# Attention, a mixture of experts and a dense layer: all engines in source order from the experts on, second-layer splits over 21 units, y's low parts on VectorE

## The chip, the cores and the metric

The kernel runs on one core of a Trainium2 chip. The metric is the device time of one execution in microseconds, the median of several runs. A core has five engines with instruction queues of their own, each of which runs its instructions in the order in which the compiled program lists them: TensorE (PE, matmuls; its weight loads are listed as PEld), VectorE (DVE), ScalarE (ACT), GpSimd (POOL) and SyncE (SP, which issues most DMAs). They wait for each other by semaphores.

## The reference

Three layers follow each other on 2 x 768 tokens of 512 numbers, all in fp32.

```python
scores_l_m = np.where(mask_l, scale * q @ k.T, -1e9)        # a window of 16 tokens
scores_s = scale * q @ k_sum.T + np.log(block)              # 24 block maxima of k
a = softmax(concatenate([scores_l_m, scores_s]))
x = a @ concatenate([v, v_sum])                             # (1536, 512)

expert_idx = np.argmax(xn @ en.T / tau, axis=1)             # 8 experts
for e in range(E):
    h = np.maximum(x[mask] @ w1[e], 0.0)                    # 512 -> 1024
    out[mask] = gate_w[mask, None] * (h @ w2[e])            # 1024 -> 512

h = np.maximum(x @ w_in, 0.0)                               # 512 -> 2048
return h * h @ w_out                                        # 2048 -> 512
```

## The kernel before

An fp32 operand of a matmul is split into a high part (rounded to fp32r) and a low part (the rest); three products of parts make up one product (`SPLIT`, `SPLIT2`). A split is always a cast on ACT and a subtraction on DVE or POOL, which needs the cast.

The kernel has three stretches. Up to about 90 us it computes the attention, whose output x is kept in `x_hl` and stored to the DRAM tile `xall`. Then come the experts. For each batch the expert that most tokens chose is applied to all tokens of the batch, 384 tokens (a group) at a time; that is `expert_units(b, gi)`. Tokens of other experts are gathered in blocks of 128: the first block is `first_block`, inside the stream; further ones would run in a loop at the end. At last comes layer two (`layer_units`), with 4 groups.

**Units.** Experts and layer two are cut into units: unit f of a group computes the first product for 128 hidden numbers (`h` or `z`, 12 matmuls), its activation (`hh` for the experts, `r` and `sq` for layer two), and the second product (`ya`, 12 matmuls, or `oa`, 9 or 12), which accumulates over f. `push(unit)` issues a unit's first half and then the second half of the unit before. So there are 16 units for each batch's experts and 64 for layer two. Counted through, units 0 to 15 belong to batch 0, 16 to 31 to batch 1, and layer two starts at 32.

**Beside the units** run generators, of which `tick()` lets each of four queues do one step, twice per unit: `route` (which expert each token takes), `plan` (the blocks), `first_block` (which calls `extra`: one-hot tiles `pt` and the sums `pi`, the gather of the rows `xe`, a transpose to `xet`, then eight steps f with `st_x`, `phe`, `he`, `ye` and `pye`) and `finish(gi)`. The last adds the block's outputs to a group's expert outputs by four matmul pairs `pd`, and makes y, layer two's input, from the sums: add on DVE (line 874), cast on ACT (875), low part on POOL (876). The banks of `pd` come from the pool `psm`, which has two.

**Layer two's weights** are 32 halves (`wm`, n = 0 to 31, two to a hidden slice). They lie in DRAM as 64-bit floats and are loaded as `sm`; DVE decodes them in three steps (lines 896, 900, 903) into `d`, and a split follows (927 on ACT, 928 on DVE). The odd halves from 9 on are decoded early and put back to DRAM (`put_by`, tile `wd`), to be loaded again as `dl` when they are split. Loads `st`, `st_x` and `sm` share the four slots of the pool `stg`.

**The order.** Two regions follow each other, attention, and the rest. In both `manual_schedule` is given PE alone: PE runs in the order of the source, and a scheduler orders the other engines by priority; `high_priority` lifts activations. `split(ns)` and `put_by(ns)` are called between units: half 0 before unit 16, halves 1 to 7 in units 16 to 22, two each in units 26 to 33 (8 to 23), and two each in units 39 to 42 (24 to 31).

Of the kernel before, what the change touches and what calls it, by code (L numbers as in the profile page):

```python
# [22 lines left out]
P = 128  # L23
# [4 lines left out]
E = 8  # L28
# [53 lines left out]
def program(ctx, tc, a):  # L82
# [411 lines left out]
    def plan():  # L494
# [15 lines left out]
        for e in range(E):  # L510
            v.tensor_tensor(
                out=st[:, e + 1 : e + 2], in0=st[:, e : e + 1], in1=nb[:, e : e + 1], op=ALU.add
            )
        cb = xt.tile([P, 24, E], F32, tag="xt", name="cb")
# [15 lines left out]
            out=rk, in0=pr, in1=st[:, :E].unsqueeze(1).to_broadcast([P, n, E]), op=ALU.add  # L530
# [3 lines left out]
        v.tensor_scalar(out=posx, in0=posx, scalar1=-1.0, scalar2=None, op0=ALU.add)  # L534
        gf = gate.rearrange("p b j -> p (b j)")
# [104 lines left out]
    region.enter_context(tc.manual_schedule(engines={ET.PE}))  # L640
# [98 lines left out]
    def extra(i, ei, pos, new, res):  # L739
# [32 lines left out]
        v.tensor_scalar(out=xe, in0=xe, scalar1=ge[:, 2:3], scalar2=None, op0=ALU.mult)  # L772
        yield 6
# [59 lines left out]
    def first_block():  # L833
# [8 lines left out]
        s.copy(ye[:, 0], pye)  # L842
        v.tensor_tensor(out=ye[:, 1], in0=pye, in1=ye[:, 0].bitcast(F32), op=ALU.subtract)
# [4 lines left out]
    def finish(gi):  # L848
# [17 lines left out]
        for m in range(NC_):  # L866
# [9 lines left out]
            g.tensor_tensor(  # L876
# [8 lines left out]

    def decoded(n):

        f, o = divmod(n, 2)
        st = stg.tile([P, DM, 2], U32, tag="stg", name=f"sm{n}")
        nc.sync.dma_start(  # L890
            st.rearrange("p n w -> p (n w)"),
            a["wm"][f].bitcast(U32)[:, o * 2 * DM : (o + 1) * 2 * DM],
        )
# [14 lines left out]
    def put_by(ns):  # L908
        for n in ns:
            words[n] = dram.tile([P, DM], U32, name=f"wd{n}")  # L910
            g.dma_start(words[n], decoded(n))

    def split(ns):

        for n in ns:
# [3 lines left out]
            if n in words:  # L919
                d = dp.tile([P, DM], U32, tag="dl", name=f"dl{n}")  # L920
                nc.sync.dma_start(d, words[n])
            else:
                d = decoded(n)
            df = d.bitcast(F32)
# [7 lines left out]
    weights(0, range(4, NF1))  # L932
# [9 lines left out]

    by = list(range(9, 2 * NF2, 2))

    def put_next():
        if by:
            put_by([by.pop(0)])

    for n, unit in enumerate(expert_units(0, 0)):
        push(unit)  # L950
        if n >= 3:
            put_next()
    while not planned:
        tick()
    X2.close()
    w1p = pool("w1p", 8, side="right")
    weights(1, range(4))
    for n, unit in enumerate(expert_units(0, 1)):
        push(unit)
        put_next()  # L960
        if 2 <= n < 6:
            weights(1, [n + 2])
    slots = [w2p] * 8 + [w1p] * 8 + [w0] * 8
    split([0])
    u1 = [expert_units(1, gi) for gi in range(2)]
    for n, unit in enumerate(u1[0] + u1[1]):
        push(unit)
        if n < 7:
            split([n + 1])
        elif n >= 10:  # L970
            split([2 * n - 12, 2 * n - 11])


    def layer_units(gi):
        st = {}

        def first(f):
# [58 lines left out]
    for n, unit in enumerate(units[:7]):  # L1036
        push(unit)
        if n < 2:
            split([2 * n + 20, 2 * n + 21])
    while queues["rows"] or queues["ends"]:  # L1040
        tick()
    Y2.close()
    w3p = pool("w3p", 8)
    for n, unit in enumerate(units[7:]):
        if n + 12 < NF2:
            split([2 * n + 24, 2 * n + 25])
        push(unit)
# [5 lines left out]
    with tc.For_i(1, n, 1) as i:  # L1053
# [7 lines left out]
        s.copy(yr, pye)  # L1061
# [90 lines left out]
```

## Time and profile before

| | |
|---|---|
| median of 3 runs | 531.59 us (530.61 to 531.60) |
| the profiled execution, its own time | 534.48 us |
| its span, first to last instruction | 532.5 us |
| mean granted clock of TensorE | 0.988 |
| PE busy | 504.7 us (95%) |
| DVE busy | 280.9 us (53%) |
| ACT busy | 196.8 us (37%) |
| POOL busy | 72.6 us (14%) |

The profile comes from one execution and gives times from the first instruction on. A timeline lists start and duration of instructions, like ones merged ("x12"); in brackets stands the idle time before them and what ended it. Instructions of one engine overlap a little in the records, so that from one start to the next is often less than the duration. A wait is put down to what came last. The granted clock is the share of TensorE's full speed that was granted.

### The profile page before, as it was taken

The numbers are of one execution on the slowest core, as the hardware profiler recorded it, in microseconds if no ns is written. First come the engines' busy times: TensorE is split into PE (matmuls) and PEld (weight loads), VectorE is DVE, ScalarE is ACT, GpSimd is POOL, SyncE is SP. The second block draws the span as 40 slices with busy tenths as digits, with TensorE's granted clock in tenths as the row PEclk, the third lists the DMA queues.
The fourth block names the chain that finished last, engine by engine and source line by source line (L and its number), as shares of the span: only waits on it lengthen the run. The fifth ranks groups of instructions, "written<-read, shape, count | busy, mean of one in ns | idle before, by whom it ended". The sixth has DMA issues, their size and how long they took to land.

```text
span 532.5 us, 9937 instructions
## 1 busy us (share of the span) xinstructions
PE 504.7 (95%) x3921; PEld 458.5 (86%) x3922; DVE 280.9 (53%) x761; ACT 196.8 (37%) x454; POOL 72.6 (14%) x77
## 2 busy tenths in 40 slices
PE   6988988999997999999999999999999999999994
PEld 3777777999996988999989999999999999999993
DVE  2875879866866769599825423222232222322221
ACT  4576678314232432344636322222222222222221
POOL 1345234010012230213202000000000000000000
PEclk9898999999998999999999999999999999999999
DMA  8945647744798657254100001000010000100001
GB/s 252 266 131 173 218 158 243 248 168 160 214 340 281 200 203 237 66 178 136 42 1 20 2 0 60 0 1 0 1 59 1 1 0 2 60 1 0 1 0 65
DMA packets 18033, 55.80 MB, mean 105 GB/s; under 512 B 2151, under 2 KB 3571, under 8 KB 17982
## 3 DMA queue, kind: packets, MB, share of 16 engines
q1 hardware_dynamic: 16942, 51.71, 30.4%
q0 software_dynamic: 1040, 3.41, 1.6%
q8 instruction: 33, 0.54, 0.4%
q14 instruction: 18, 0.15, 0.1%
HBM read 45.66 MB, written 9.44 MB: 103 GB/s over the span
## 4 chain that ended last, share of the span: by engine, by line
PE 73%; DVE 10%; DMA 8%; ACT 4%; issue 2%; POOL 1%; SPq 1%; ACTq 0%; DVEq 0%; POOLq 0%
PE z L656 25%; PE oa L1010 25%; PE ya L701 7%; PE h L656 7%; DMA sm<-wm 4%; ACT sc L339 2%; DMA qk<-qk 2%; DVE d L900 1%; PE pq L318 1%; DVE d L903 1%; DVE w L287 1%; PE pa L364 1%; DMA st<-we 1%; DMA xe<-xall,idx 1%; PE pe L349 1%
## 5 line engine op out<-in xcount | busy, mean ns | idle before, releaser
L656 PE MATMUL z<-y,wm 128*128 128x384 f32 x768 | 144.2, 336 | 0.0
L1010 PE MATMUL oa<-wm,sq 128*128 128x512 f32 (+1 forms) x624 | 143.2, 376 | 0.0
L656 PEld LDWEIGHTS z<-y,wm 128*128 128x128 f32 x768 | 134.5, 188 | 3.7
L1010 PEld LDWEIGHTS oa<-wm,sq 128*128 128x128 f32 x624 | 111.6, 188 | 18.4 <-DVE sq L989 0.3
L988 DVE TENSOR_TENSOR r<-r 128x384 f32<-128x384 f32 x56 | 31.3, 558 | 155.7 <-ACT sq L984 155.7
L983 ACT ACTIVATE r<-z 128x384 f32<-128x384 f32 x64 | 31.4, 491 | 178.3 <-PE z L656 178.2
L701 PE MATMUL ya<-hh,w 128*128 128x384 f32 x384 | 74.6, 343 | 1.3 <-DVE hh L688 1.0
L656 PE MATMUL h<-x,w 128*128 128x384 f32 x384 | 73.6, 339 | 0.0
L701 PEld LDWEIGHTS ya<-hh,w 128*128 128x128 f32 x384 | 68.7, 192 | 2.4 <-DVE hh L688 1.3
L656 PEld LDWEIGHTS h<-x,w 128*128 128x128 f32 x384 | 67.0, 188 | 0.5
L989 DVE TENSOR_TENSOR sq<-r,sq 128x384 fp32r<-128x384 f32 x64 | 37.1, 580 | 12.9 <-ACT r L986 7.7
L339 ACT ACTIVATE sc<-sc,mx 128x120 f32<-128x120 f32 x96 | 30.2, 385 | 21.5 <-DVE mx L334 19.0
L984 ACT ACTIVATE sq<-r 128x384 fp32r<-128x384 f32 x64 | 33.6, 524 | 2.0
L687 ACT ACTIVATE hh<-h 128x384 fp32r<-128x384 f32 x32 | 15.7, 490 | 40.1 <-PE h L656 38.2
L876 POOL TENSOR_TENSOR y<-yt,y 128x384 fp32r<-128x384 f32 x16 | 18.4, 1152 | 68.6 <-ACT y L875 68.5
L903 DVE SCALAR_TENSOR_TENSOR d<-sm,d 128x512 uint32<-128x512 uint32 x32 | 25.1, 788 | 0.3
L896 DVE TENSOR_SCALAR d<-sm 128x512 uint32<-128x512 uint32 x32 | 16.1, 506 | 17.0 <-DMA sm<-wm 14.9
L334 DVE CUSTOM_DVE_ANT_0 sc<-pq,mask 128x120 f32<-128x120 f32 x96 | 20.8, 277 | 3.6 <-PE pq L318 3.5
L900 DVE SCALAR_TENSOR_TENSOR d<-sm,d 128x512 uint32<-128x512 uint32 x32 | 21.8, 687 | 0.4
L688 DVE SCALAR_TENSOR_TENSOR hh<-h,hh 128x384 fp32r<-128x384 f32 x32 | 17.6, 552 | 7.5 <-ACT hh L687 7.3
L286 ACT CAST w<-st 128x512 fp32r<-128x512 f32 x28 | 16.0, 624 | 15.0 <-DMA st<-we 15.0
L318 PE MATMUL pq<-qk 64*64 64x96 f32 x384 | 17.3, 263 | 4.1 <-DVE mx L334 2.0
(172 smaller groups left out, 477.6 us busy)
## 6 DMA issues: line engine op xcount, KB each, us to landing
sm<-wm SPq DMA_DIRECT2D x32, 512.0 KB, 4.5
st<-we SPq DMA_DIRECT2D x16, 512.0 KB, 4.7
qk<-qk SPq DMA_DIRECT2D x7, 768.0 KB, 9.6
vt<-vw SPq DMA_DIRECT2D x8, 648.0 KB, 7.3
st_x<-we SPq DMA_DIRECT2D x8, 512.0 KB, 4.4
xall<-xr SPq DMA_DIRECT2D x4, 768.0 KB, 5.3
wd<-d POOLq DMA_DIRECT2D x12, 256.0 KB, 5.0
dl<-wd SPq DMA_DIRECT2D x12, 256.0 KB, 2.7
```

Source lines behind the costliest of these rows:

```text
L318: t.matmul(pq[hh][o * D : (o + 1) * D, k, 96 * part : (96, KW)[part]], qk[rows, QAT + w * D : QAT + (w + 1) * D], km[rows] if part else qk ...
L334: v.tensor_tensor_reduce(out=sc[:, k], in0=pq[hh][:, k], in1=mask[:, kind], op0=ALU.add, op1=ALU.min, scale=-0.125, scalar=3e38, accum_out ...
L339: s.activation(out=sc[:, k], in_=sc[:, k], func=AF.Exp, bias=mx[:, k : k + 1], scale=-1.0)
L656: t.matmul(ps, W[:, i, c * P : (c + 1) * P], xg[:, k, c, :], start=(n == 0), stop=(n == 11))
L701: t.matmul(st["acc"][m], W[b][f][1][:, i, m * P : (m + 1) * P], hh[:, k], start=(f == 0 and i == k == 0), stop=(f == NF1 - 1 and (i, k) == ...
L900: v.scalar_tensor_tensor(out=d, in0=hw, scalar=0xC0000000, in1=d, op0=ALU.bitwise_and, op1=ALU.bitwise_or)
L903: v.scalar_tensor_tensor(out=d, in0=lw, scalar=29, in1=d, op0=ALU.logical_shift_right, op1=ALU.bitwise_or)
L983: s.activation(out=r, in_=ps, func=AF.Relu)
L984: s.activation(out=hh[:, 0], in_=r, func=AF.Square)
L988: v.tensor_tensor(out=r, in0=r, in1=r, op=ALU.mult)
L989: v.tensor_tensor(out=hh[:, 1], in0=r, in1=hh[:, 0].bitcast(F32), op=ALU.subtract)
L1010: t.matmul(st["acc"][q], hh[:, i, k * P : (k + 1) * P], WM[f][1][:, j, c0:c1], start=(f == 0 and i == j == 0), stop=(f == NF2 - 1 and (j, ...
```

## The change

- The second region is given all five engines: PE, DVE, ACT, POOL and SP now run in the order of the source. `high_priority` does nothing there.
- What is done beside the units stands in a table: `at(u, fn, ...)` puts a call into unit u, and `run(u)` makes the calls of unit u after its `push`. Loads and their use are separate now (`fetch` and `decoded`; `weight_load` and `weight_split`), with the load one unit ahead of its use. Halves 0 to 7 are split in units 16 to 23, halves 8 to 31 in units 26 to 44, by one or two. Odd halves from 9 on are put by in units 4, 5, 6, 7, 8, 10, 12, 14, 18, 20, 24 and 25. Weights 5 to 7 of batch 0 and all of batch 1 come one per unit.
- The low parts of y go from POOL to DVE.
- `extra` no longer multiplies the gathered rows by the gate; the gate is a factor where the block's output is copied. A pause of 6 ticks becomes 5 and 1, with the first load of `st_x` between, and each later `st_x` is issued a step ahead.
- `plan` copies its sums out of the bank (`prs`) and gets three pauses; in `experts` a pause of 6 becomes 5.
- In layer two's first group all 16 units have their second square on ACT (8 before).

```diff
-    region.enter_context(tc.manual_schedule(engines={ET.PE}))
+    region.enter_context(
+        tc.manual_schedule(engines={ET.PE, ET.DVE, ET.Activation, ET.Pool, ET.SP})
+    )
...
-        v.tensor_scalar(out=xe, in0=xe, scalar1=ge[:, 2:3], scalar2=None, op0=ALU.mult)
-        yield 6
+        yield 5
+        def load(f):
+            st = new("st", [P, 2 * DM], F32)
+            nc.sync.dma_start(st, a["we"][bass.ds(ei, 1), f].rearrange("o p n -> (o p) n"))
+            return st
+        ahead_st = load(0)
+        yield
...
-                st = new("st", [P, 2 * DM], F32)
-                nc.sync.dma_start(st, a["we"][bass.ds(ei, 1), f].rearrange("o p n -> (o p) n"))
+                st = ahead_st
+                if f < NF1 - 1:
+                    ahead_st = load(f + 1)
...
-        s.copy(ye[:, 0], pye)
-        v.tensor_tensor(out=ye[:, 1], in0=pye, in1=ye[:, 0].bitcast(F32), op=ALU.subtract)
+        gt = ex["ge"][:, 2:3]
+        s.activation(out=ye[:, 0], in_=pye, func=AF.Copy, scale=gt)
+        v.scalar_tensor_tensor(
+            out=ye[:, 1], in0=pye, scalar=gt, in1=ye[:, 0].bitcast(F32),
+            op0=ALU.mult, op1=ALU.subtract,
+        )
...
             s.copy(y[:, 0, m], yf)
-            g.tensor_tensor(
+            v.tensor_tensor(
                 out=y[:, 1, m], in0=yf, in1=y[:, 0, m].bitcast(F32), op=ALU.subtract
             )
...
+    def fetch(n):
+        if n in words:
+            st = staged[n] = dp.tile([P, DM], U32, tag="dl", name=f"dl{n}")
+            nc.sync.dma_start(st, words[n])
+        else:
+            f, o = divmod(n, 2)
+            st = staged[n] = stg.tile([P, DM, 2], U32, tag="stg", name=f"sm{n}")
...
+    def at_weights(b, f, u):
+        at(u - 1, weight_load, b, f)
+        for o in range(2):
+            at(u, weight_split, b, f, o)
...
+    for n, u in zip(range(9, 2 * NF2, 2), (4, 5, 6, 7, 8, 10, 12, 14, 18, 20, 24, 25)):
+        at(u - 1, fetch, n)
+        at(u, put_by, n)
+    for n in range(2 * NF2):
+        f, o = divmod(n, 2)
+        if f < 4:
+            u = U1 + n
+        else:
+            u = o + U1 + 10 + (0, 2, 3, 5, 6, 8, 9, 11, 13, 14, 16, 17)[f - 4]
+        at(u - 1, fetch, n)
+        at(u, split, [n])
...
-        if n < 7:
-            split([n + 1])
-        elif n >= 10:
-            split([2 * n - 12, 2 * n - 11])
+        run(U1 + n)
...
-                if gi == 0 and f < 8:
+                if gi == 0:
                     s.activation(out=r, in_=r, func=AF.Square)
```

Three places of the compiled order follow, before and after (line numbers of the two kernels differ). In the names, `sq01` is group 0, f = 1; `yt10` the sum of batch 1, group 0, `pd20` the addition to it.

VectorE at the first two units of layer two, before:

```order
L989 TENSOR_TENSOR sq00_3518<-r00_3517,sq00_3518 128x384
L719 TENSOR_TENSOR yt11_3535<-ya111_3198,srow11_3358 128x384
L719 TENSOR_TENSOR yt11_3535<-ya113_3200,srow11_3358 128x384
L874 TENSOR_TENSOR yt10_3162<-yt10_3162,pd20_3543 128x384
L724 TENSOR_TENSOR yt11_3535<-yt11_3535,srow11_3358 128x384 x2
L928 TENSOR_TENSOR wm23_3617<-dl23_3615,wm23_3617 128x512
L874 TENSOR_TENSOR yt10_3162<-yt10_3162,pd21_3582 128x384
L989 TENSOR_TENSOR sq01_3577<-r01_3576,sq01_3577 128x384
```

and after:

```order
L1039 TENSOR_TENSOR sq00_3490<-r00_3489,sq00_3490 128x384
L726 TENSOR_TENSOR yt11_3507<-ya111_3187,srow11_3338 128x384
L726 TENSOR_TENSOR yt11_3507<-ya113_3189,srow11_3338 128x384
L731 TENSOR_TENSOR yt11_3507<-yt11_3507,srow11_3338 128x384 x2
L954 TENSOR_TENSOR wm15_3514<-dl15_3472,wm15_3514 128x512
L927 TENSOR_SCALAR d16_3517<-sm16_3474 128x512
L931 SCALAR_TENSOR_TENSOR d16_3517<-sm16_3474,d16_3517 128x512
L934 SCALAR_TENSOR_TENSOR d16_3517<-sm16_3474,d16_3517 128x512
L954 TENSOR_TENSOR wm16_3521<-d16_3517,wm16_3521 128x512
L1039 TENSOR_TENSOR sq01_3540<-r01_3539,sq01_3540 128x384
L893 TENSOR_TENSOR yt10_3143<-yt10_3143,pd20_3546 128x384
```

The adds of `pd20` and `pd21` stood ahead of `sq01`; now a short split, a decode and its split stand between `sq00` and `sq01`, and the add of `pd20` behind it, with y's low part behind that.

ScalarE at the same place, before:

```order
L983 ACTIVATE r00_3517<-z00_3504 128x384
L984 ACTIVATE sq00_3518<-r00_3517 128x384
L986 ACTIVATE r00_3517<-r00_3517 128x384
L721 COPY yt11_3535<-ya110_3197 128x384
L721 COPY yt11_3535<-ya112_3199 128x384
L927 CAST wm23_3617<-dl23_3615 128x512
L875 CAST y2_3542<-yt10_3162 128x384
L983 ACTIVATE r01_3576<-z01_3563 128x384
```

and after:

```order
L1033 ACTIVATE r00_3489<-z00_3476 128x384
L1034 ACTIVATE sq00_3490<-r00_3489 128x384
L1036 ACTIVATE r00_3489<-r00_3489 128x384
L728 COPY yt11_3507<-ya110_3186 128x384
L728 COPY yt11_3507<-ya112_3188 128x384
L953 CAST wm15_3514<-dl15_3472 128x512
L953 CAST wm16_3521<-d16_3517 128x512
L1033 ACTIVATE r01_3539<-z01_3526 128x384
```

Between `r00` and `r01` there is now the cast `wm16`, whose decode `d16` stands on VectorE behind the `yt` steps, and y's cast has gone behind `r01`.

SyncE at the steps f = 4 and 5 of the first block (ISA rows compute an address), before:

```order
L890 DMA sm2_2824<-wm 128x1024
L709 DMA srow10_3011<-srow1_77 128x384
L786 ISA
L786 DMA st_x_2849<-we 128x1024
L786 ISA
L786 DMA st_x_2876<-we 128x1024
L890 DMA sm3_2891<-wm 128x1024
```

and after:

```order
L915 DMA sm25_2773<-wm 128x1024
L915 DMA sm2_2782<-wm 128x1024
L783 ISA
L783 DMA st_x_2800<-we 128x1024
L783 ISA
L783 DMA st_x_2827<-we 128x1024
L915 DMA sm3_2855<-wm 128x1024
```

Two loads of halves, `sm25` and `sm2`, now stand ahead of `st_x` of step 4 where one stood.

## Rows read from the trace of the kernel before

**Rows 1.** By stretch: us busy (PE, PEld, DVE, ACT, POOL), granted clock, DMA share, GB/s

```profile
210.00:253.00 43.00, 43.00 (x251) 42.68 (x250) 36.72 (x60) 17.38 (x34) 10.13 (x8) 1.00 0.43 138
...
168.70:172.60 3.90, 3.87 (x14) 3.54 (x13) 0.95 (x3) 0.91 (x3) 0.00 (x0) 0.57 0.95 355
```

**Rows 2.** Who PE waited for: engine, line, releaser: us in total, times, longest

```profile
PE phe L789 <- ACT xet L778: 2.3, 1, 2.3
...
PE ya L701 <- DVE hh L688: 1.0, 1, 1.0
...
PE pye L803 <- POOL ye L810: 0.9, 1, 0.9
PE pi L758 <- DVE pt L752: 0.9, 2, 0.6
...
PE pye L803 <- ACT ye L809: 0.5, 1, 0.5
...
PE ya L701 <- ACT hh L687: 0.3, 1, 0.3
```

**Rows 3.** PE's timeline, first extra block: start us, us, instruction, [idle before]

```profile
168.70 3.87 PE L701 MATMUL ya<-hh,w 128*128 128x384 f32 x12
...
176.60 1.05 PE L789 MATMUL phe<-xet,st_x 128*128 128x128 f32 x8
...
180.31 1.05 PE L789 MATMUL phe<-xet,st_x 128*128 128x128 f32 x8
```

**Rows 4.** The tile st_x: its instructions with ns (least, median, most), time to landing

```profile
L786 SPq DMA_DIRECT2D st_x<-we x8: 332/336/343, 161.4 to 188.6; - x8
L809 ACT CAST ye<-st_x x8: 610/622/623, 165.3 to 198.9; 128x512 fp32r<-128x512 f32 x8
L810 POOL TENSOR_TENSOR ye<-st_x,ye x8: 1297/1307/1697, 166.0 to 199.5; 128x512 fp32r<-128x512 f32 x8
...
DMA to landing us min/median/max: 4.2/4.4/5.5
```

**Rows 5.** DVE's timeline in units 20 to 29, and one wait for ACT

```profile
189.29 0.69 DVE L928 TENSOR_TENSOR wm<-d,wm 128x512 fp32r<-128x512 f32 x1 [0.69 <-ACT wm L927]
...
233.00 0.43 DVE L896 TENSOR_SCALAR d<-sm 128x512 uint32<-128x512 uint32 x1
233.46 0.69 DVE L900 SCALAR_TENSOR_TENSOR d<-sm,d 128x512 uint32<-128x512 uint32 x1
234.19 0.69 DVE L903 SCALAR_TENSOR_TENSOR d<-sm,d 128x512 uint32<-128x512 uint32 x1
234.80 0.55 DVE L688 SCALAR_TENSOR_TENSOR hh<-h,hh 128x384 fp32r<-128x384 f32 x1
235.27 0.68 DVE L928 TENSOR_TENSOR wm<-dl,wm 128x512 fp32r<-128x512 f32 x1
235.87 0.68 DVE L928 TENSOR_TENSOR wm<-d,wm 128x512 fp32r<-128x512 f32 x1
```

**Rows 6.** A decode's third step on DVE, and POOL's y step beside it (timeline)

```profile
239.18 1.50 DVE L903 SCALAR_TENSOR_TENSOR d<-sm,d 128x512 uint32<-128x512 uint32 x1
...
238.83 1.31 POOL L876 TENSOR_TENSOR y<-yt,y 128x384 fp32r<-128x384 f32 x1 [10.39 <-ACT y L875]
```

**Rows 7.** ACT's timeline, first unit of layer two (relu, then the second square)

```profile
255.49 0.49 ACT L983 ACTIVATE r<-z 128x384 f32<-128x384 f32 x1 [1.47 <-PE z L656]
...
256.57 0.53 ACT L986 ACTIVATE r<-r 128x384 f32<-128x384 f32 x1
```

**Rows 8.** The chain that ended last: start us, us, what

```profile
257.91 2.08 PE z L656 x12
260.33 2.07 PE oa L1010 x9
```

**Rows 9.** DVE's first decode behind the stores of x, and `ya` of unit 2

```profile
98.97 0.43 DVE L896 TENSOR_SCALAR d<-sm 128x512 uint32<-128x512 uint32 x1 [0.63 <-DMA sm<-wm]
...
101.01 2.24 PE L701 MATMUL ya<-hh,w 128*128 128x384 f32 x12
```

More of the change, by code (lines that the diff above doesn't have):

```diff
@@ L499, in plan @@
             t.matmul(pr[:, k:], ones, ohx[:, : n - k], start=False, stop=(k == n - 1))
+        prs = xt.tile([P, n, E], F32, tag="xt", name="prs")
+        v.tensor_copy(prs, pr)
         pc = psm.tile([P, E], F32, tag="m", name="pcx")
@@ L513, in plan @@
             )
+        yield
         cb = xt.tile([P, 24, E], F32, tag="xt", name="cb")
@@ L529, in plan @@
         v.tensor_tensor(
-            out=rk, in0=pr, in1=st[:, :E].unsqueeze(1).to_broadcast([P, n, E]), op=ALU.add
+            out=rk, in0=prs, in1=st[:, :E].unsqueeze(1).to_broadcast([P, n, E]), op=ALU.add
         )
@@ L534, in plan @@
         v.tensor_scalar(out=posx, in0=posx, scalar1=-1.0, scalar2=None, op0=ALU.add)
+        yield
         gf = gate.rearrange("p b j -> p (b j)")
@@ L771, in extra @@
         )
-        v.tensor_scalar(out=xe, in0=xe, scalar1=ge[:, 2:3], scalar2=None, op0=ALU.mult)
-        yield 6
+        yield 5
+        def load(f):
[3 more added lines that the diff above has]
+        ahead_st = load(0)
+        yield
         px = psm.tile([P, NC_, P], F32, tag="m", name="pxe")
@@ L884, in program @@
     words = {}
-    def decoded(n):
[L888 to L893, printed above, removed]
+    staged = {}
+    def fetch(n):
[5 more added lines that the diff above has]
+            st = staged[n] = stg.tile([P, DM, 2], U32, tag="stg", name=f"sm{n}")
+            nc.sync.dma_start(
+                st.rearrange("p n w -> p (n w)"),
+                a["wm"][f].bitcast(U32)[:, o * 2 * DM : (o + 1) * 2 * DM],
+            )
+    def decoded(n):
+        st = staged.pop(n)
+        if n in words:
+            return st
         lw, hw = st[:, :, 0], st[:, :, 1]
@@ L906, in decoded, with put_by @@
         return d
[L908 to L911, printed above, removed]
+    def put_by(n):
+        d = decoded(n)
+        words[n] = dram.tile([P, DM], U32, name=f"wd{n}")
+        g.dma_start(words[n], d)
     def split(ns):
@@ L918, in split @@
                 WM.append([])
[L919 to L924, printed above, removed]
+            df = decoded(n).bitcast(F32)
             wp = slots[n] if n < 24 else w3p
@@ L929, in split, with at, run @@
             WM[f].append(w)
-    weights(0, range(4, NF1))
+    beside = {}
+    def at(u, fn, *args):
+        beside.setdefault(u, []).append((fn, args))
+    def run(u):
+        for fn, args in beside.pop(u, []):
+            fn(*args)
+    def at_weights(b, f, u):
+        at(u - 1, weight_load, b, f)
+        for o in range(2):
+            at(u, weight_split, b, f, o)
+    U1, U2 = 2 * NF1, 4 * NF1
+    at(-1, weight_load, 0, 4)
+    for f in range(4, NF1):
+        if f < NF1 - 1:
+            at(f - 4, weight_load, 0, f + 1)
+        for o in range(2):
+            at(f - 4, weight_split, 0, f, o)
+    for f in range(NF1):
+        at_weights(1, f, NF1 + f)
+    for n, u in zip(range(9, 2 * NF2, 2), (4, 5, 6, 7, 8, 10, 12, 14, 18, 20, 24, 25)):
[9 more added lines that the diff above has]
+        at(u, split, [n])
+    run(-1)
     for b in range(B):
@@ L941, in program @@
     later("rows", first_block())
[L943 to L947, printed above, removed]
     for n, unit in enumerate(expert_units(0, 0)):
         push(unit)
[L951 to L957, printed above, removed]
+        if n == NF1 - 1:
+            while not planned:
+                tick()
+            X2.close()
+            w1p = pool("w1p", 8, side="right")
+        run(n)
     for n, unit in enumerate(expert_units(0, 1)):
         push(unit)
-        put_next()
-        if 2 <= n < 6:
-            weights(1, [n + 2])
+        run(NF1 + n)
     slots = [w2p] * 8 + [w1p] * 8 + [w0] * 8
-    split([0])
     u1 = [expert_units(1, gi) for gi in range(2)]
@@ L1035, in program @@
         tick()
-    for n, unit in enumerate(units[:7]):
-        push(unit)
[L1038 to L1047, printed above, removed]
+    for n, unit in enumerate(units):
+        if n == 7:
+            while queues["rows"] or queues["ends"]:
+                tick()
+            Y2.close()
+            w3p = pool("w3p", 8)
+        push(unit)
+        run(U2 + n)
     push(None)
@@ L1060, in program @@
         yr = new_loop("yr", [P, DM], F32)
-        s.copy(yr, pye)
+        s.activation(out=yr, in_=pye, func=AF.Copy, scale=ge[:, 2:3])
         pt = psm.tile([P, NC_, P], F32, tag="m", name="pyt")
```

## The prediction

> **What bounds the kernel now.** I read the busy times by stretch first: from 210 to 253 us TensorE (PE) is busy for all 43 us, VectorE (DVE) for 36.7 [rows 1], and it stays so to the end. A change that neither adds nor removes matmuls can only win what PE waits for, or lose by making it wait. Next I read who PE waited for [rows 2]. What matters lies between 140 and 202 us: 0.9 us for the one-hot tiles `pt`, 1.0 and 0.3 for `hh` of one expert unit, 2.3 in the first extra block (`phe`), 0.5 and 0.9 at its end (`pye`). Last, PE's timeline behind the 2.3 us: twelve `ya` matmuls take 3.87 us there [rows 3], 1.6 over the 2.24 of the twelve at 101 us [rows 9], and the granted clock of that stretch is 0.57 against 1.00 [rows 1]: PE was mostly on its lower level, 1.2 of 2.4 GHz. All of it: 0.9 + 1.3 + 2.3 + 1.6 + 1.4 = 7.5 us. That is all there is to win.
>
> Then I asked what would be late in the new order. The diff puts DVE, ScalarE (ACT), GpSimd (POOL) and SyncE (SP) in the order of the source. Before, only PE was, and DVE began the decode of a later half while ACT was casting an earlier one.
>
> **What goes away.** The waits for `hh` (1.3 us) came when ACT and DVE waited for late weight loads; in the new order each load is issued a unit or more ahead: gone. The gather's multiply by the gate leaves DVE's row, and `pxe` and `phe` now have twelve `h` or twelve `ya` ahead of them, 2.1 us each [rows 8], which hide ACT's copy to `xet`: 2.3 and the slow clock's 1.6 gone. The gate returns as a factor in two instructions that exist already: nothing. The twelve compares for `pt` come in two lots of six, still behind an `hh`; of the 0.9 us I take 0.3 as won, between 0 and 0.9.
>
> **The first block gets a new wait.** Weight tiles of all kinds share four slots (`stg`). The new order puts `sm25`, `sm2`, `sm3`, `sm27` and `sm4` between the block's eight loads, so `st_x` of step f+2 starts only when step f's tile is released, or behind another that waits for that. From `phe` of step f this is 1.6 us for `phe` and `pye` (a step of 3.71 [rows 3] less twelve matmuls), before which the single `ye` may not be overwritten, 0.65 for ACT's cast, 1.33 for POOL's subtraction, 0.35 for the issue of a load ahead of it in SP's row and 4.4 for landing [rows 4]: 8.35 us. PE is back for f+2 after two steps: 7.4. So some 0.95 us is lost up to three times (steps 2, 4, 6): 2.8 us. Its bounds are 0 (a slot comes free one step earlier than I count) and 6 (each load lands in 5.5, the most of this block's). So the block gives 2.3 + 1.6 + 1.4 - 2.8 = 2.5 us.
>
> Won in all: 0.3 + 1.3 + 2.5 = 4.1 us.
>
> **What the splits cost in order.** Take DVE's starts one behind another [rows 5]: decode 0.46 + 0.73 + 0.69 us; then ACT's cast, for which DVE stood 0.69 us where nothing else could go ahead; then the subtraction, 0.60. In the new order nothing else ever goes ahead: 3.17 us for a split with decode, 2.5 of it work. A half that was decoded earlier costs 0.6 to 0.75. `hh`, `sq` and each of four `yt` steps take 0.47, as the `hh` row does; `pm` 0.53. For y's low part on DVE the trace has no row; the nearest is `hh`, of the same shape: 0.47, and no more than the 0.69 of the longest step of a decode. But it stands behind ACT's cast too: add 0.55, hand-over and cast 0.57 (the square of rows 7 and 0.04), low part 0.47, which is 1.6 us for each of 16. A price below nothing would need POOL's instruction, now gone, to have cost DVE more than that: it held it for 0.81 us where they met [rows 6].
>
> In layer two ACT's order matters as well: a unit's relu, square and square take 1.61 us [rows 7] behind the cast of the split before, so DVE's `sq` comes 1.65 us after that cast, and DVE is idle for 1.0 of them.
>
> A unit is one first half (`h` or `z`) and one second (`ya` or `oa`), 4.2 us of PE; units 16 to 31 are the second batch's experts, 32 is the first of layer two. Up to unit 27 the order fits: the largest, unit 24, has 2 x 1.6 + 1.9 + 1.8 + 0.5 = 7.4 us of DVE, which 4.9 us of PE and the 2.4 us that `hh` may be late cover. From `pd10`, behind unit 28, it doesn't.
>
> *To `pd22`, behind z02 of unit 34.* DVE, from the end of `pd10` to the first add of y2: four splits 12.7, four y steps 6.4, three short splits 2.1, three `hh` 1.4, `pm` 0.5, two `sq` 0.9, `yt` 1.9, two waits for ACT 2.0, add 0.55: 28.5 us. PE in the same piece: six first halves and four `ya` at 2.08, one `oa` 2.07, five `pd` at 0.35, `pp` 0.15 [rows 8]: 24.8. `pd22` takes the bank of `pd20`, which that add frees. PE stands 3.7 us, some of it already at `ya` of unit 30.
>
> *To `oa` of unit 35.* DVE and ACT from that add: four y steps, a short split, the wait for `sq`, a decode, cast, relu, square: 12.15 us. PE: 0.6 until it may start, then 9.15. It stands 2.4 us.
>
> *To `oa` of unit 36.* 5.8 us (`sq`, `pm`, a short split, decode to square) against 4.15: 1.65 us.
>
> *To `pd33`.* That needs y3's second add, which stands behind a split and behind `sq` of unit 38: 10.0 us against 7.25: 2.75 us. Unit 41 loses 0.7 more; after that only two units in three have a decode, and PE leads.
>
> Lost in all: 3.7 + 2.4 + 1.65 + 2.75 + 0.7 = 11.2 us.
>
> **Costed at nothing.** Weights 5 to 7 of the first batch are now issued behind the last store of x. The first load behind that store had landed by 98.97 us; two casts and a relu, 1.7 us, make `hh002` ready at 100.7, and PE's `ya` wants it at 101.01 [rows 9]. Price 0, and up to 2 us if that thin cover is gone. SP reads three registers between the second batch's loads: under the last rival. The step of `experts()` that comes a tick earlier, the copy `prs` and three pauses in `plan` lie beside matmuls. ACT's squares for the rest of the first group replace DVE's only after the tight units: nothing.
>
> **Sum.** The profiled execution took 534.48 us (its span 532.5 and 2.0 around it), 2.9 above the median of the runs, 531.59. On its own scale 534.5 - 4.1 + 11.2 = 541.6; on that of the median 538.7.
>
> **A rule weighed.** The row shows it first: the decode's third step takes 1.50 us instead of 0.69 when POOL's y step runs beside it [rows 6]. The Trainium skill (SBUF — State Buffer, "Who interferes with whom") says that a VectorE instruction with two SBUF inputs and a GpSimd instruction that reads SBUF exclude each other, the later one blocking fully. The trace agrees, with 0.81 us. By that rule the unblocked times that I used stay right and the sum is 538.7; if the 1.50 has another cause that stays, some three such rows in the tight units make it 541.1.
>
> **The rivals.** *DVE keeps up (18%).* Freed of POOL's blocks [rows 6], DVE and ACT run their row in less time than I add up. It decides when the first piece's 28.5 us come down to PE's 24.8, an eighth less; by the same factor the other pieces lose 0.9, 0.9 and 1.5 us, 3.3 in all, and the kernel takes 531.6 - 4.1 + 3.3 = 530.8; a fifth less, with the block's loads in time too, gives about 526. For it: DVE still had 6.3 us to spare in 43 before, with POOL in its way, and PE never stood [rows 1]. Against it: much of my sum is hand-over from ACT, which no faster DVE removes. *Gain and loss cancel (8%)*, 531.6: the block free of its new wait (2.8) and the 11.2 down to 7. *Late loads too (10%).* The four slots and SP's register reads also hold up the second batch's weights until PE stands as in the 2.3 us gap; two or three such gaps give 543 to 546. That the orders don't change is excluded: the compiled rows show it.
>
> **How the numbers follow.** Forecast 64%: 538.7, itself 534 to 543. Slower 74% (forecast and late loads), faster 18%, within 0.2% (1.06 us, about what a measurement can tell) 8%. The range of 529.5 to 544 leaves out the lower half of the first rival and the far end of the last. If PE's clock falls again behind a gap, that mostly eats into the next gap, since DVE is what is late; only behind the last does it add up to 1.6.
>
> **What would show it.** Right: PE idle before `pd` and `oa` in the first ten units of layer two, with DVE or ACT as releaser; about 1 us before two or three `phe`; none before `hh` of unit 14; 3.1 to 3.2 us on DVE from a decode's start to its subtraction's end. Wrong: PE without a wait from unit 28 to 41, or a loss that lies before unit 16.

## The result and the profile after

The changed kernel took 536.27 us (median of 4 runs, 536.07 to 538.88) against 531.1 us (4 runs, 529.5 to 531.6) for the kernel before: slower, with a ratio of 1.0114, 95% interval 1.0075 to 1.0153. The forecast was 538.7 us, slower.

The profiled execution took 536.43 us, its span 534.6. All of TensorE's waits behind the attention stand in four rows of the list of who PE waited for (engine, line, releaser: us in total, times, longest). They answer to [rows 2]:

```profile
PE pd L888 <- DVE yt L893: 4.7, 2, 2.6
PE phe L804 <- DMA st_x<-we: 4.7, 2, 2.5
...
PE oa L1060 <- ACT sq L1034: 1.5, 2, 1.2
...
PE ya L708 <- ACT hh L694: 0.4, 1, 0.4
```

The rows of [rows 2], 5.9 us, are gone; 11.3 us of others have come, seven waits. All seven are at places that the prediction named: `phe` of steps 4 and 6, `ya` of unit 30, `pd22`, `oa` of units 35 and 36, `pd33`. The last five in PE's timeline (start us, us, instruction, idle before it and what ended that; the wait of unit 30, 0.43 us at 243.15, is left out):

```profile
259.21 0.62 PE L888 MATMUL pd<-pm,ye 128*128 128x384 f32 x2 [2.59 <-DVE yt L893]
259.67 3.57 PE L1060 MATMUL oa<-wm,sq 128*128 128x512 f32 x9
...
265.75 2.21 PE L1060 MATMUL oa<-wm,sq 128*128 128x512 f32 x9
...
270.56 2.35 PE L1060 MATMUL oa<-wm,sq 128*128 128x512 f32 x9 [0.27 <-ACT sq L1034]
...
276.22 2.36 PE L1060 MATMUL oa<-wm,sq 128*128 128x512 f32 x9 [1.22 <-ACT sq L1034]
...
285.98 0.61 PE L888 MATMUL pd<-pm,ye 128*128 128x384 f32 x2 [2.13 <-DVE yt L893]
286.43 3.12 PE L663 MATMUL z<-y,wm 128*128 128x384 f32 x12
```

Two of them left more behind than idle time. The nine `oa` at 259.67 took 3.57 us against 2.21 at 265.75, and behind `pd33` the `z` took 3.12. Busy times by stretch (us; PE, PEld, DVE, ACT, POOL; granted clock, DMA share, GB/s) give the clock:

```profile
259.67:263.24 3.57, 3.57 (x11) 2.80 (x11) 2.24 (x4) 2.42 (x6) 0.00 (x0) 0.58 0.00 0
286.43:292.17 5.74, 5.74 (x22) 5.19 (x22) 3.57 (x7) 3.02 (x7) 0.00 (x0) 0.70 0.30 101
265.75:267.80 2.05, 2.05 (x10) 1.50 (x9) 1.44 (x4) 0.51 (x1) 0.00 (x0) 1.00 0.14 56
```

The granted clock was 0.58 and 0.70 there, so PE was for the greater part on 1.2 GHz, and 1.00 between.

Why `pd22` waited is read from VectorE's timeline in units 32 and 33:

```profile
254.07 0.42 DVE L927 TENSOR_SCALAR d<-sm 128x512 uint32<-128x512 uint32 x1
254.53 0.69 DVE L931 SCALAR_TENSOR_TENSOR d<-sm,d 128x512 uint32<-128x512 uint32 x1
255.25 0.69 DVE L934 SCALAR_TENSOR_TENSOR d<-sm,d 128x512 uint32<-128x512 uint32 x1
256.63 0.69 DVE L954 TENSOR_TENSOR wm<-d,wm 128x512 fp32r<-128x512 f32 x1 [0.69 <-ACT wm L953]
258.13 0.56 DVE L1039 TENSOR_TENSOR sq<-r,sq 128x384 fp32r<-128x384 f32 x1 [0.81 <-ACT r L1036]
258.61 0.55 DVE L893 TENSOR_TENSOR yt<-yt,pd 128x384 f32<-128x384 f32 x1
259.73 0.56 DVE L895 TENSOR_TENSOR y<-yt,y 128x384 fp32r<-128x384 f32 x1 [0.58 <-ACT y L894]
260.21 0.55 DVE L893 TENSOR_TENSOR yt<-yt,pd 128x384 f32<-128x384 f32 x1
```

A decode of 1.87 us, 0.69 idle for the cast, the subtraction, 0.81 idle until ACT's second square, `sq`, and only then the add (258.61) that frees the bank of `pd20`; PE went on at 259.21. From 254.07 to the end of the subtraction are 3.25 us. The forecast counts from start to start, and so does a split further up: from 232.69, its decode's start, to the next instruction at 235.86 are 3.17 us, the forecast's number. The y step, from one add (258.61) to the next (260.21), takes 1.60 us, as forecast, 0.58 of them idle.

To compare the two executions I took the start of each first half on PE, counted from the first full `h` behind the attention (90.49 us before, 85.52 after). Up to unit 9 they agree within 0.01 us. When the first block is done the changed kernel is 3.6 us ahead, from unit 30 on it falls back, by `z` of unit 40 it is 7.5 behind, and so it stays to the end: 11.1 us were lost in between. The rest of the account lies in the attention, below.

### The profile page after: what moved, and what is told of

Read it like the earlier page. It is cut to its first block, busy times and chain, and to the rows that moved or that the text cites. A ratio compares the mean times of both kernels' runs of the same rounds, so it can differ in the third digit from the quotient of the medians.

```text
span 534.6 us, 9909 instructions
## 1 busy us (share of the span) xinstructions
PE 505.5 (95%) x3921; PEld 458.8 (86%) x3922; DVE 285.8 (53%) x769; ACT 200.0 (37%) x462; POOL 54.2 (10%) x61
## 4 chain that ended last, share of the span: by engine, by line
PE 71%; DVE 11%; ACT 8%; DMA 4%; issue 2%; POOL 1%; SPq 0%; ACTq 0%; POOLq 0%
PE oa L1060 23%; PE z L663 22%; PE ya L708 10%; PE h L663 10%; ACT sc L339 2%; DMA st_x<-we 2%; DMA vt<-vw 2%; DVE d L931 1%; DVE d L934 1%; ACT wm L953 1%; PE pl L434 1%; DVE sc L334 1%; DVE yt L893 1%; PE pq L318 1%; DVE x L388 1%
## 5 line engine op out<-in xcount | busy, mean ns | idle before, releaser
L1060 PE MATMUL oa<-wm,sq 128*128 128x512 f32 (+1 forms) x624 | 145.4, 379 | 1.5 <-ACT sq L1034 1.5
L1060 PEld LDWEIGHTS oa<-wm,sq 128*128 128x128 f32 x624 | 113.0, 190 | 21.0 <-ACT sq L1034 2.1
L1038 DVE TENSOR_TENSOR r<-r 128x384 f32<-128x384 f32 x48 | 26.8, 558 | 137.6 <-ACT sq L1034 137.6
L708 PE MATMUL ya<-hh,w 128*128 128x384 f32 x384 | 73.4, 338 | 0.5 <-ACT hh L694 0.4
L708 PEld LDWEIGHTS ya<-hh,w 128*128 128x128 f32 x384 | 67.2, 188 | 1.6 <-ACT hh L694 0.6
L1039 DVE TENSOR_TENSOR sq<-r,sq 128x384 fp32r<-128x384 f32 x64 | 35.7, 558 | 25.3 <-ACT r L1036 20.2
L953 ACT CAST wm<-d 128x512 fp32r<-128x512 f32 x20 | 12.4, 621 | 58.7 <-DVE d L934 58.7
L934 DVE SCALAR_TENSOR_TENSOR d<-sm,d 128x512 uint32<-128x512 uint32 x32 | 25.1, 784 | 1.1
L931 DVE SCALAR_TENSOR_TENSOR d<-sm,d 128x512 uint32<-128x512 uint32 x32 | 23.1, 723 | 1.1
L287 DVE TENSOR_TENSOR w<-st,w 128x512 fp32r<-128x512 f32 x28 | 20.0, 752 | 3.3 <-ACT w L286 3.2
L954 DVE TENSOR_TENSOR wm<-d,wm 128x512 fp32r<-128x512 f32 x20 | 13.9, 693 | 13.7 <-ACT wm L953 13.7
```

The lines of the kernel that those rows point to most:

```text
L708: t.matmul(st["acc"][m], W[b][f][1][:, i, m * P : (m + 1) * P], hh[:, k], start=(f == 0 and i == k == 0), stop=(f == NF1 - 1 and (i, k) == ...
L931: v.scalar_tensor_tensor(out=d, in0=hw, scalar=0xC0000000, in1=d, op0=ALU.bitwise_and, op1=ALU.bitwise_or)
L934: v.scalar_tensor_tensor(out=d, in0=lw, scalar=29, in1=d, op0=ALU.logical_shift_right, op1=ALU.bitwise_or)
L1038: v.tensor_tensor(out=r, in0=r, in1=r, op=ALU.mult)
L1039: v.tensor_tensor(out=hh[:, 1], in0=r, in1=hh[:, 0].bitcast(F32), op=ALU.subtract)
L1060: t.matmul(st["acc"][q], hh[:, i, k * P : (k + 1) * P], WM[f][1][:, j, c0:c1], start=(f == 0 and i == j == 0), stop=(f == NF2 - 1 and (j, ...
```

## The experiments

All kernels are the changed one with an edit, but for two that start from the kernel before. "Shift" is the time from the first full `h` behind the attention to the last matmul of the profiled execution, less that of the changed kernel; it leaves the attention out. Ratios are to the kernel before on the same chip; the changed kernel's is 1.0114, its shift 0, and the shift of the kernel before is -7.5. The expectations are in us for a chip on which the kernel before takes 531.1; on the chips of these runs it took 531.4, 532.5 or 532.7. So a time is held against its band "by ratio", as the ratio times 531.1.

| run | median us | ratio, 95% interval | shift us |
|---|---|---|---|
| pe_order_only | 529.44 | 0.993 (0.9903 to 0.9957) | -8.2 |
| decode_ahead | 528.6 | 0.9921 (0.9887 to 0.9955) | -9.9 |
| late_low | 532.19 | 0.9999 (0.9977 to 1.0022) | -5.0 |
| y_low_pool | 534.61 | 1.0037 (1.0012 to 1.0063) | -5.7 |
| before_low_dve | 532.62 | 1.0017 (0.9989 to 1.0044) | -7.0 |
| fifth_slot | 536.33 | 1.0075 (1.004 to 1.0109) | -2.0 |
| block_clear | 541.21 | 1.0169 (1.0136 to 1.0202) | +3.4 |
| before_pause5 | 529.8 | 0.996 (0.9939 to 0.9981) | -5.6 |
| pause6 | 540.97 | 1.0149 (1.0113 to 1.0186) | +0.8 |
| all_mends | 526.47 | 0.9902 (0.9864 to 0.994) | -11.0 |
| tuned | 522.09 | 0.9794 (0.9767 to 0.9821) | -16.1 |

### Is it the order, or the amount of work?

```diff
-    region.enter_context(
-        tc.manual_schedule(engines={ET.PE, ET.DVE, ET.Activation, ET.Pool, ET.SP})
-    )
+    region.enter_context(tc.manual_schedule(engines={ET.PE}))
```

> The changed kernel with the order of the source for TensorE alone, the other engines ordered by the scheduler as in the kernel before; table of halves, low parts of y on VectorE, the gate's new place stay. Theory (waiting in order): the scheduler puts other work ahead of what waits for a cast; TensorE's waits between 240 and 290 us go, and the time is 526 to 529 us. Rival (the table's places for the splits, and y's low parts as work, are what make VectorE late): the waits at pd stay, 535 to 537 us.

No wait at `pd` or `oa` is left, with the same table and the same instructions. By ratio it takes 527.4 us, inside the band. In the profiled executions it is 2.9 us behind the changed kernel up to unit 31, by waits between units 10 and 26, and wins 11.0 from there to unit 40, where the changed kernel loses its 11.1. The order alone, given the table, costs 1.8%. The parts of the change that no run takes singly (the gate's place, the loads of `st_x` a step ahead, `prs` and the pauses in `plan`, the squares on ACT) are all in this kernel, which is 0.7% faster than the kernel before.

```diff
-        if n in words:
+        if n in words or n in ready:
             return st
...
+    def decode(n):
+        d = decoded(n)
+        staged[n] = d
+        ready.add(n)
...
-        at(u - 1, fetch, n)
+        if n % 2 and n >= 9:
+            at(u - 1, fetch, n)
+        else:
+            at(u - 2, fetch, n)
+            at(u - 1, decode, n)
         at(u, split, [n])
```

> The changed kernel with each decode issued one unit ahead of its split (its load two units ahead), so that the cast has its input when ScalarE comes to it; nothing is left out. Theory (waiting in order): a split with decode takes VectorE 2.5 us in place of 3.17, and ScalarE's relu no longer stands behind a cast that waits for VectorE; the waits at oa (0.3, 1.2) and at pd (2.6, 2.1) go but for under 1 us: about 529.5 us, and VectorE is idle for under 0.1 us before each subtraction. Rival (amount of work): 535 to 537 us. If the loads that come earlier take slots from the block's loads, phe waits longer than the 4.7 us of the changed kernel and some of the gain is lost.

Here the order stays the source's, and only what stands behind what is changed. All of the waits at `pd` and `oa` but 0.2 us went, and by ratio it takes 526.9 us, better than forecast. VectorE at the same place as above, timeline of this kernel:

```profile
251.51 0.68 DVE L961 TENSOR_TENSOR wm<-dl,wm 128x512 fp32r<-128x512 f32 x1
252.12 0.68 DVE L961 TENSOR_TENSOR wm<-d,wm 128x512 fp32r<-128x512 f32 x1
253.36 0.56 DVE L1050 TENSOR_TENSOR sq<-r,sq 128x384 fp32r<-128x384 f32 x1 [0.56 <-ACT r L1047]
253.83 0.55 DVE L893 TENSOR_TENSOR yt<-yt,pd 128x384 f32<-128x384 f32 x1
```

The two subtractions follow each other without a wait, and the add stands at 253.83, where the changed kernel had 258.61. Of the 0.81 us before `sq`, 0.56 are left. The waits at `phe` came to 3.4 us, so in sum the earlier loads did not lengthen the block's waits.

```diff
             s.copy(y[:, 0, m], yf)
-            v.tensor_tensor(
-                out=y[:, 1, m], in0=yf, in1=y[:, 0, m].bitcast(F32), op=ALU.subtract
-            )
+            for j in ([m - 1] if m else []) + ([m] if m == NC_ - 1 else []):
+                v.tensor_tensor(
+                    out=y[:, 1, j], in0=yu[gi][:, j], in1=y[:, 0, j].bitcast(F32), op=ALU.subtract
+                )
```

> The changed kernel with y's low part issued on VectorE one step later, behind the add of the next step; nothing is left out. Theory (waiting in order): a y step costs VectorE 1.60 us after the change because 0.58 us of it are spent waiting for the cast on ScalarE; with the low part a step later it costs some 1.0 us. TensorE's waits at pd of 2.6 and 2.1 us (records of the changed kernel) shrink to under 1 us together, the 0.3 us at oa goes, the 1.2 us at oa of unit 36 stays: about 531 us. Rival (amount of work): VectorE has the same instructions to do and is late by their number; 535 to 537 us, the waits at pd as before.

Where two steps meet, no wait is left between add and low part (VectorE's timeline):

```profile
236.95 0.54 DVE L893 TENSOR_TENSOR yt<-yt,pd 128x384 f32<-128x384 f32 x1
237.41 0.55 DVE L896 TENSOR_TENSOR y<-yt,y 128x384 fp32r<-128x384 f32 x1
237.88 0.55 DVE L893 TENSOR_TENSOR yt<-yt,pd 128x384 f32<-128x384 f32 x1
238.34 0.55 DVE L896 TENSOR_TENSOR y<-yt,y 128x384 fp32r<-128x384 f32 x1
239.52 0.69 DVE L955 TENSOR_TENSOR wm<-dl,wm 128x512 fp32r<-128x512 f32 x1 [0.63 <-ACT wm L954]
```

A step takes 0.93 us. But behind it stands a split whose cast has y's cast ahead of it on ACT, and VectorE waits 0.63 us there instead. The waits at `pd` fell to 2.4 us, not to under 1, and the 1.2 at `oa` stayed; the time, 531.0 us by ratio, is as expected.

### y's low parts

```diff
-            v.tensor_tensor(
+            g.tensor_tensor(
                 out=y[:, 1, m], in0=yf, in1=y[:, 0, m].bitcast(F32), op=ALU.subtract
             )
```

> The changed kernel with one part undone: y's low parts on GpSimd again, everything else as changed, nothing left out. Theory (waiting in order): VectorE's y step falls from 1.60 us to the add alone, 0.5 us, plus up to 0.8 us where GpSimd's step holds one of its instructions up; the waits at pd (2.6 and 2.1 us) fall to under 1.5 us together, those at oa (0.3, 1.2) stay: 530 to 533 us. Rival (the low parts are better on VectorE, since GpSimd holds it up for as long as it frees it): waits as before, 535.5 to 538 us.

By ratio it takes 533.1 us (531.7 to 534.4), at the upper end of the theory's band, but not in the theory's way: the waits at `pd` hardly moved (4.4 us after 4.7), which is what the rival had said. The rows of the first y steps tell why (timelines of VectorE, ScalarE and GpSimd):

```profile
235.49 1.01 DVE L893 TENSOR_TENSOR yt<-yt,pd 128x384 f32<-128x384 f32 x2
237.60 0.69 DVE L954 TENSOR_TENSOR wm<-dl,wm 128x512 fp32r<-128x512 f32 x1 [1.10 <-ACT wm L953]
238.21 1.24 DVE L927 TENSOR_SCALAR d<-sm 128x512 uint32<-128x512 uint32 x1
236.07 0.98 ACT L894 CAST y<-yt 128x384 fp32r<-128x384 f32 x2 [1.30 <-DVE yt L893]
236.96 0.61 ACT L953 CAST wm<-dl 128x512 fp32r<-128x512 f32 x1
236.66 2.50 POOL L895 TENSOR_TENSOR y<-yt,y 128x384 fp32r<-128x384 f32 x2 [3.48 <-ACT y L894]
```

Two adds in 1.01 us, as hoped. Then VectorE waits 1.10 us for the cast of `wm` (236.96), which stands behind the two casts of y; and the next decode step takes 1.24 us instead of 0.42, because GpSimd's steps run beside it. Taking an instruction out of a row that runs in order moved the wait to the next one that needs ACT. Of the shift of -5.7, 1.3 lie in the first block, and some 1.6 in the clock, which stayed at 1.00 behind `pd33` here.

```diff
-            g.tensor_tensor(
+            v.tensor_tensor(
                 out=y[:, 1, m], in0=yf, in1=y[:, 0, m].bitcast(F32), op=ALU.subtract
```

> The kernel before with one part of the change alone: y's low parts on VectorE; the scheduler still orders VectorE, ScalarE, GpSimd and SyncE. Theory (waiting in order): the low part goes in behind other work, costs VectorE 0.47 to 0.56 us with no wait for the cast, and VectorE has that to spare: within 1 us of the kernel before, no wait of TensorE over 0.5 us at pd or oa. Rival (the low parts as work are what makes VectorE late): 16 of them with hand-over, 3 to 6 us slower, with waits at pd.

From 200 us on this kernel's PE has one wait, 0.9 us at the block's last `pye`. Low parts on VectorE are no loss where the scheduler fills the hand-over: no difference that can be measured.

### The first block

The rows of the changed kernel first (timelines of PE, VectorE, GpSimd and SyncE, 176 to 187 us):

```profile
176.54 1.13 PE L804 MATMUL phe<-xet,st_x 128*128 128x128 f32 x8 [2.12 <-DMA st_x<-we]
178.02 0.29 DVE L811 SCALAR_TENSOR_TENSOR he<-phe,he 128x128 fp32r<-128x128 f32 x1 [4.65 <-ACT he L810]
178.22 0.42 DVE L927 TENSOR_SCALAR d<-sm 128x512 uint32<-128x512 uint32 x1
178.68 0.69 DVE L931 SCALAR_TENSOR_TENSOR d<-sm,d 128x512 uint32<-128x512 uint32 x1
179.40 1.68 DVE L934 SCALAR_TENSOR_TENSOR d<-sm,d 128x512 uint32<-128x512 uint32 x1
179.14 1.40 POOL L825 TENSOR_TENSOR ye<-st_x,ye 128x512 fp32r<-128x512 f32 x1 [4.72 <-ACT ye L824]
180.56 0.34 SPq L915 DMA_DIRECT2D sm<-wm  x1
181.14 2.09 SPq L783 DMA_DIRECT2D st_x<-we  x2
186.72 1.13 PE L804 MATMUL phe<-xet,st_x 128*128 128x128 f32 x8 [2.54 <-DMA st_x<-we]
```

Behind `phe` of step 4 and `pye` come ACT's cast and GpSimd's subtraction `ye` (179.14). At its end (180.54) a slot is free for the load of a half, `sm`, which SyncE issues at 180.56. `st_x` of step 6 stands behind it in SyncE's row and follows at 181.14, 0.58 us later; in the kernel before a load `st_x` that waited for nothing followed the one ahead of it by 0.57 (177.24 to 177.81). `phe` starts at 186.72. That is a loop of 10.2 us; PE would be back in two steps of 3.8. The loop from step 2 to step 4 is the same, with 9.8 us (166.78 to 176.54). VectorE's decode behind `he` comes close: its third step takes 1.68 us instead of 0.69 beside `ye` and ends at 181.08, so that an earlier end of `ye` would win little unless the decode ended earlier too.

```diff
+    turn = {"n": 0}
...
         if kind == "st":
+            turn["n"] += 1
+            if turn["n"] % 2 == 0:
+                return y2.tile(shape, dt, tag="stx", name="st_x", bufs=1)
             return stg.tile(shape, dt, tag="stg", name="st_x")
+        if kind in ("xe", "xet"):
+            return yp.tile(shape, dt, tag="yt", name=kind)
```

> The changed kernel with a fifth slot for weight tiles, used by every second load of the first extra block (room for it comes from keeping xe and xet in tiles of the pool yp); nothing is left out. Theory (slots): the two waits of 2.1 and 2.5 us at phe come from loads that wait for a slot which a decode on VectorE releases; with a fifth slot both fall under 0.5 us, and the time to about 531.5 us. Rival (transfers): the loads land late because the DMA engines are full (5.1 us to landing, 4.4 before); both waits stay within 0.5 us, 536 us.

The rows above show the release at GpSimd, and the decode beside it. The run itself is inconclusive, by a flaw of the edit. The fifth slot was tied to the odd steps, so the load of step 3 had to wait for step 1 to be done, with all of SyncE's row behind it. SyncE's timeline:

```profile
156.77 12.43 SPq L783 DMA_DIRECT2D st_x<-we  x2
```

The second load of that row ends its issue 12.4 us after the first began. The waits at `phe` came to 3.4 us (on DMA and on VectorE). Of the shift of -2.0 the block has 0.6; the rest is the clock behind `pd33` again.

```diff
-    for n, u in zip(range(9, 2 * NF2, 2), (4, 5, 6, 7, 8, 10, 12, 14, 18, 20, 24, 25)):
+    for n, u in zip(range(9, 2 * NF2, 2), (4, 5, 6, 7, 8, 9, 10, 11, 12, 13, 14)):
...
-            u = U1 + n
+            u = (16, 17, 21, 22, 23, 24, 25, 25)[n]
```

> The changed kernel with the loads of halves moved out of the first extra block: odd halves 9 to 29 are put by in units 4 to 14 (31 is decoded when it is split), halves 2 to 7 are split in units 21 to 25; nothing is left out. Theory (slots): the loads st_x then have three or four slots to themselves, both waits at phe (2.1 and 2.5 us in the changed kernel) fall under 0.5 us, and nothing else changes by over 1 us: 531 to 533 us. Rival (the step of the block itself is too long: he on VectorE and ye on GpSimd in order, or landing): the waits stay, 536 us.

The step of the block is as the theory has it: with the slots to itself `phe` waits 0.4 us, and the block gains 5.0, so the loads of halves in SyncE's row made the wait. But "nothing else changes" was wrong, and the time, 540.1 us by ratio, lies in neither band. Who PE waited for:

```profile
PE ya L708 <- ACT hh L694: 5.2, 2, 4.8
...
PE pi L765 <- DVE pt L759: 2.1, 1, 2.1
...
PE phe L804 <- DMA st_x<-we: 0.4, 1, 0.4
```

Decodes in units 9 to 11 stand ahead of the `pt` tiles, and two splits in unit 25 ahead of `hh` of unit 26, whose `ya` came 4.8 us late. The same work put elsewhere in a row that runs in order cost more than it won: 3.4 us by the shift (by the ratios 1.0169 after 1.0114, whose intervals overlap a little).

### The attention

The pause of 6 ticks in `experts()`, 5 after the change, was costed at nothing.

```diff
-        yield 6
+        yield 5
         v.reciprocal(out=rxt, in_=rxt)
```

> The kernel before with one part of the change alone: the pause in experts() is 5 instead of 6, so that the four matmuls pn come a tick earlier in the attention. Theory (the attention gained from it): the wait of 1.7 us before pn goes, the attention ends 1.5 to 2.5 us earlier than in the kernel before, and the time falls by as much, to 529 or 530.5 us. Rival (the profiled execution of the kernel before was a slow one in its attention, and the pause does nothing): no difference that can be measured.

> The changed kernel with one part undone: the pause in experts() is 6 again; nothing is left out. Theory (the attention gained from the shorter pause): a wait of 1.7 us before pn comes back, the attention ends 1.5 to 2.5 us later than in the changed kernel, 538 to 539 us. Rival (it does nothing): 536 to 536.5 us, and no wait before pn.

The first confirms it: 0.4% faster, clear of noise. Undone in the changed kernel, the ratio rises by as much, from 1.0114 to 1.0149; these two intervals overlap, so there it is the row of the wait that shows it. With the pause of 6 the list of waits has a row that neither kernel with 5 has:

```profile
PE pn L258 <- ACT mb L199: 1.7, 1, 1.7
```

The list of the kernel before has it too. In the profiled executions the attention ends at 85.5 to 86.7 us in nine of the ten kernels with a pause of 5 (89.5 in the last below, where PE waited 2.7 us for a load of `qk`), and at 88.4, 89.1 and 90.5 in the three with a pause of 6. By the ratios some 2 us were won.

### All mends

> The changed kernel with three edits together: decode one unit ahead of its split, y's low part one step later, and the loads of halves out of the first extra block; nothing is left out. Theory: the losses are separate waits, so the gains add up: 4.7 us at phe (with some 0.5 of slow clock) and all of the waits at pd and oa with their slow clock; 523 to 525 us, and no wait of TensorE over 0.5 us behind the attention. Rival (VectorE has too much to do): a wait at pd or oa of over 1 us stays, 527 us or more.

The edits are `decode_ahead`, `late_low` and `block_clear` together. It gained, though less than forecast (525.9 us by ratio). At `phe`, `pd` and `oa` nothing is left; what is, block_clear had brought:

```profile
PE pi L765 <- DVE pt L759: 2.2, 1, 2.2
...
PE ya L708 <- DVE hh L695: 0.8, 1, 0.8
```

Behind `pi` 4.2 us were lost in all, the slow clock included.

```diff
-    for n, u in zip(range(9, 2 * NF2, 2), (4, 5, 6, 7, 8, 9, 10, 11, 12, 13, 14)):
+    for n, u in zip(range(9, 24, 2), (4, 5, 6, 7, 8, 10, 12, 14)):
...
-            u = (16, 17, 21, 22, 23, 24, 25, 25)[n]
+            u = (16, 17, 18, 21, 22, 23, 24, 25)[n]
...
+            u = n + 15
```

> The changed kernel with decode one unit ahead of its split, y's low part one step later, and another table: halves 9 to 23 odd are put by in units 4, 5, 6, 7, 8, 10, 12 and 14, halves 25 to 31 odd are not put by but decoded for their split, splits 0 to 7 in units 16, 17, 18 and 21 to 25, 24 to 31 one per unit in units 39 to 46; nothing is left out. Theory (separate waits): against the kernel with all three mends, the waits of 2.2 us at pi and 0.8 us at ya with the slow clock behind them go (4.2 and 1.0 us together) and nothing new comes, since VectorE is then no longer asked for a decode while pt is wanted: 521 to 522.5 us. Rival (VectorE is now late where it decodes without a break, units 38 to 46): a wait of over 1 us at oa or z there, 524 us or more.

The diff is against `all_mends`, as far as the table goes; its last line is for halves 24 to 31. As the theory has it, between 92 us and the end TensorE waits for nothing. By ratio the kernel takes 520.2 us, a little less than forecast: 2.1% faster than the kernel before and 3.2% faster than the changed one. Busy times from its page (us, share of the span, instructions):

```profile
PE 501.8 (96%) x3922; PEld 456.4 (87%) x3922; DVE 284.8 (54%) x769; ACT 201.5 (39%) x462; POOL 51.8 (10%) x57
```

VectorE does hardly less than in the changed kernel (285.8), so the amount of its work was not what made it late.

## Why the prediction was right, point by point

- **What goes away.** Forecast 1.3 (`hh`), 0.3 (`pt`) and 2.5 in the block; 3.6 us were won for 4.1. The `hh` waits went, and so did all of the 0.9 us for `pt`, the upper bound. That leaves 1.4 for the block: its new waits took 4.7 us where I had 2.8.
- **The block's new wait.** The mechanism was right: four slots, GpSimd's subtraction as the releaser, and `st_x` behind another load in SyncE's row. The size was off: 9.8 and 10.2 us for 8.35, and two waits for up to three. In the second loop it is 2.60 us to GpSimd's start (forecast 2.25), 1.40 for the subtraction (1.33), 0.60 to the issue of `st_x` (0.35) and 5.58 from there to `phe` (4.4). Why loads landed later than before these runs do not settle. The decode that ends within 0.1 us of that issue was not in the forecast.
- **The splits in order.** 3.25 us for 3.17, and 1.60 for 1.6. From the add behind `pd10` to the end of y2's first add VectorE took 28.1 us (231.08 to 259.16) for a forecast of 28.5. PE's waits by then were 0.4 and 2.6, for 3.7.
- **The later waits.** 0.3, 1.2 and 2.1 us against 2.4, 1.65 and 2.75; the 0.7 of unit 41 did not come. The waits from unit 30 on sum to 6.6, not to 11.2. Yet 11.1 were lost, since PE was slow behind two of them: 1.4 us at `oa` (3.57 less 2.21) and 0.3 at `pd23`, and 1.6 behind `pd33` (`z` 3.12 and `oa` 2.99, 2.25 each at full speed). That a slow clock eats into the next gap was in the prediction. `fifth_slot` has the other half of it: its clock stayed up behind `pd22` (2.21 us for the nine `oa`), and the next gaps at `oa` came to 1.9 us in place of 1.5, with the slow clock behind them (3.69 us for the nine `oa` of unit 35); by unit 38 it had nothing left of its lead. Only behind the last gap is the clock a loss of its own: in `fifth_slot`, `pause6` and `y_low_pool` it did not fall there, and each won 1.6 us on the changed kernel at that place. With the clock up, then, the loss is 9.5 us for a forecast of 11.2; that 11.1 came so close is in part luck. Of the remaining 1.2 us most lies at the waits themselves, since PE's instructions overlap a little and cannot at a wait: `tuned`, which has none of them, takes 10.8 us less than the changed kernel between units 31 and 40, for 9.9 us of waits and slow clock.
- **The rule weighed.** A decode step takes 1.68 us in place of 0.69 wherever GpSimd's `ye` runs beside it (176 to 181 us), and one took 1.24 in place of 0.42 beside y's step in `y_low_pool`. By the Trainium skill (SBUF — State Buffer, "Who interferes with whom") the two engines share a pair of ports, and whoever comes second is blocked fully; the trace agrees, with 1.0 and 0.8 us in these rows, and at 181.08 the held step ends 0.54 us after GpSimd's. The change did free VectorE of this in layer two, and it was worth less than the hand-over that it brought: `y_low_pool`, which takes both back, is 0.8% faster than the changed kernel, a part of it by the clock.
- **Costed at nothing.** The early loads cost nothing, as said. The pause in `experts()` was wrong: I had it beside matmuls, but the row of PE's wait before `pn` in the attention (1.7 us) was not looked at. It is most of the 2.4 us by which the forecast was too slow; with the 2 us the sum is 536.7. "All there is to win" left it out for the same reason.
- **The rivals.** That VectorE keeps up is refuted by 28.1 us. That gain and loss cancel needed a block without its new wait, which took 4.7 us. Late weight loads of the second batch did not occur.

So the account closes: 3.6 us won and 11.1 lost behind the attention, some 2 won in it, 5.5 us in all, for a difference of 5.2 between the medians. The two profiled executions differ by more in the attention, 5.0 us; the executions with one and the same pause are up to 2.1 (pause of 6) and 4.0 us (pause of 5) apart there, so what exceeds the 2 us is not put down to the change. The second part of the kernel before is not fixed to the microsecond, though: it was 0.5 us longer in `before_low_dve` and 2.0 in `before_pause5`, by longer waits between units 10 and 20.

## What to carry to other kernels

Before an engine is put in the order of the source, look for every instruction whose operand another engine must first make from this engine's last result: each such pair cost its hand-over in full here, and what took it away was to write the second half one step later. Moving work elsewhere helped only where the new place had room. So treat the places of the work as a budget for each unit, since what moves out of one tight unit falls on another. And read the waits of the whole kernel, also of stages that a change seems only to brush.

## What was not expected of the hardware

PE's clock behind a wait of the same length is not the same: in the changed kernel 2.59 us at `pd22` were followed by a granted clock of 0.58 for 3.6 us, while 2.58 to 2.68 us at the same place were followed by 1.00 in `y_low_pool`, `fifth_slot`, `block_clear` and `pause6` (nine `oa` in 2.21 to 2.24 us). A shorter wait can cost the clock too: 1.88 us at `oa` of unit 35 in `fifth_slot`. What decides it these runs do not show.
